# GpSimd forms the low mantissa bits of eleven weight tiles, and the second chunk's first layer is issued ahead of the first chunk's second layer

## The chip, the cores and the metric

The kernel runs on one core of one Trainium2 chip. The metric is the device time of one execution in microseconds (us); the lower the better. The core's engines are named as the profile names them: PE (TensorE, with PEld for its weight loads), DVE (VectorE), ACT (ScalarE), POOL (GpSimd), and SP, which only issues DMAs here. Each engine takes its instructions strictly in the order in which they were written for it.

## What is computed

Attention with a local window and global tokens, then a gated feed-forward layer ("MoE" in the names, though there is one expert):

```python
# batch 8, heads 8, 512 local + 32 global tokens, head size 64
s_g  = q_g @ concat(k_g, k_l).T / 8          # global queries see all keys
s_ll = where(|i - j| <= 32, q_l @ k_l.T / 8, -1e9)
s_l  = concat(q_l @ k_g.T / 8, s_ll)         # local queries: window + global keys
out  = concat(softmax(s_g) @ v, softmax(s_l) @ v)
x    = out as 4608 tokens x 512
xn   = x / sqrt(mean(x*x) + 1e-6) * rms_g
y    = (silu(xn @ w_gate) * (xn @ w_val)) @ w_out     # 512 -> 2 x 1536 -> 512
```

The attention inputs are float32. The three weight matrices are float64 and reach the chip as raw 64-bit words.

## The kernel before, in words

**Chunks.** The tokens are worked on in nine chunks: chunk c (0 to 7) is the 512 local tokens of batch c, chunk 8 all 256 global tokens. A chunk needs its attention, its root-mean-square norm, its first layer (the products with w_gate and w_val, in 12 slices f of 128 columns) and its second layer (the product with w_out). Matrix products of the feed-forward part are made in float16 with each operand split into a high and a low half, three products for one. Chunks 2 to 8 use fewer products, with sums of weight blocks ("folds") that the kernel forms once during chunks 0 and 1, stores to DRAM and fetches for each chunk. Chunks 0 and 1 use the weights as they lie in SBUF.

**Weights.** The 18 tiles of weights (0 to 11: slices of w_gate and w_val; 12 to 17: w_out) are turned from float64 into two float16 halves on the chip, each by this chain, in which the letter is the step's name in the order and the number behind it the tile:

- W: two DMAs of 512 KB each bring the raw 64-bit words.
- m (`rebias`): two instructions of 128x512 multiply the upper word, read as a float32, by 2^-112, on DVE for the tiles in `MULT_V` and on ACT for the others.
- s (`shift`): DVE shifts all 1024 words left by 3.
- the three lowest bits, from the lower word's upper half (two instructions of 128x512 16-bit numbers with a step of 8 bytes): step k (`three`) on ACT for the tiles in `LOW_A`, step l (`low`) on DVE for the others.
- g (`sign`): two DVE instructions of 128x512 put sign, shifted word and the three bits together. Their two inputs both lie in SBUF.
- q: ACT squares the tile and sums the squares; p: PE adds these sums up; e: some small DVE instructions make the tile's power-of-two scales from them (for two tiles at a time from tile 2 on: p2 and e2 are of tiles 2 and 3, p3 and e3 of tiles 4 and 5, and so on).
- a: ACT writes the high half (128x1024); d: DVE writes the low half (128x1024).

**The first chunks' other steps.** Attention unit u (0 to 3 belong to chunk 0, 4 to 7 to chunk 1): L and V load it, S makes the scores on PE, M (eight DVE instructions of 128x128) adds the mask and takes the maximum, E (eight on ACT) the exponentials, T (PE) and C (ACT) turn them round, A (PE) multiplies by the values, R and X (DVE) divide, Q (ACT) squares, Z (DVE) sums squares. Then for chunk 0 or 1: N (13 small DVE instructions in a chain: the inverse root), D (four on DVE), U (PE turns and scales the tokens, four parts), H (ACT) and Y (DVE) the high and low halves. I f.wi: first-layer products of chunk 0, slice f, matrix w, half i (six matmuls of 128x512); B (ACT tanh), b, h (DVE) the gate, c (ACT) and r (DVE) its two halves; O i.j: second-layer products of chunk 0, o its results. J, j, u, w: folds. K: the scale of w_out. Steps with a leading 1 (1:P0 to 1:P71, R, w) are those of chunk 1: P0 to P47 are its first layer, P48 to P71 its second. Steps such as 1:S/0+1 are attention of a later chunk.

**Order.** `JOBS` lists the steps of chunk 0 as they are set up; the program first only notes every instruction under a name like `0:M2.1.3` (chunk:step.part). Then

```python
    for name in ORDER.split() or list(plan):
        for call in plan.pop(name):
            call()
```

writes all 3692 noted parts in the order of the list `ORDER`, which was made ahead of time and stands in the file. What `ORDER` says for one engine is that engine's queue. `PAGES` and `BANKS` say in the same manner which of the 43 SBUF pages (128x1024 floats), 8 wide ones and 8 PSUM banks each tile takes. A tile framework adds the waits between engines.

Of the kernel before, what the change touches and what calls it, by code (L numbers as in the profile page):

```python
# [71 lines left out]
0:l1.1 0:g1.0 0:g1.1 0:q1.0 0:z3.0 0:z4.1 0:T3.1.0 0:z4.0 0:R0.0 0:S1.0 0:M1.0.3 0:M1.0.1 0:M1.0.0
0:M1.0.2 0:V2.0 0:M1.1.1 0:M1.1.0 0:C2.1.0 0:M1.1.2 0:E1.0.0 0:M1.1.3 0:z4.2 0:R2.0 0:z2.2 0:m0.0
0:m0.1 0:s0.0 0:A0.0 0:l0.0 0:m3.0 0:E1.1.0 0:g0.0 0:m3.1 0:k3.0 0:l0.1 0:T1.1.0 0:V1.0 0:T1.0.0
0:p1.0 0:A2.0 0:s3.0 0:X0.0 0:g3.0 0:C1.0.0 0:Q0.0 0:g0.1 0:q0.0 0:T3.0.0 0:C1.1.0 0:g3.1 0:V3.0
0:X2.0 0:z2.3 0:p0.0 0:e0.0 0:e0.1 0:e0.2 0:z5.0 0:C3.0.0 0:Q2.0 0:z6.0 0:W2.0 0:C3.1.0 0:e1.0
0:q3.0 0:R3.0 0:A1.0 0:R1.0 0:Z0.0 0:e1.1 0:z6.1 0:W4.0 0:Z2.0 0:z6.2 0:X1.0 0:A3.0 0:a0.0 0:X3.0
0:Q1.0 0:e1.2 0:L4.0 0:Z1.0 0:Q3.0 0:Z3.0 0:N0.0.0 0:N0.1.0 0:N0.2.0 0:N0.3.0 0:N0.4.0 0:N0.5.0
0:N0.6.0 0:m2.0 0:s2.0 0:N0.7.0 0:k2.0 0:N0.8.0 0:N0.9.0 0:N0.10.0 0:N0.11.0 0:N0.12.0 0:g2.0 0:D0.1
0:W7.0 0:a1.0 0:D0.2 0:D0.3 0:m4.0 0:W5.0 0:W6.0 0:D0.0 0:U0.3.0 0:U0.0.0 0:d0.0 0:g2.1 0:e0.3  # L80
0:s4.0 0:U0.1.0 0:k4.0 0:d1.0 0:g4.0 0:q2.0 0:H0.1.0 0:U0.2.0 0:H0.0.0 0:g4.1 0:m7.1 0:S4.0 0:m5.0
0:k5.0 0:Y0.1.0 0:q4.0 0:Y0.0.0 0:H0.3.0 0:e1.3 0:p2.0 0:m7.0 0:H0.2.0 0:M4.0.0 0:e2.0 0:M4.0.2
0:e2.1 0:a2.0 0:m6.0 0:s7.0 0:s5.0 0:e0.4 0:g5.1 0:e2.3 0:k6.0 0:L5.0 0:g5.0 0:q5.0 0:Y0.3.0
# [18 lines left out]
0:d11.0 0:g12.0 0:g12.1 0:I10.00.0 0:V7.0 0:I10.01.0 0:b8.0 0:I11.00.0 0:C4.0.0 0:k16.0 0:h8.0
0:q12.0 0:g14.0 0:B9.0 0:R4.0 0:B10.0 0:s16.0 0:g16.0 0:K0.1 0:g17.1 0:q17.0 0:S7.0 0:b9.0 0:g16.1
0:e6.5 0:I11.10.0 0:b10.0 0:C4.1.0 0:M7.1.3 0:q16.0 0:g14.1 0:M7.0.1 0:M7.1.2 0:I11.01.0 0:I10.10.0
0:I10.11.0 0:I11.11.0 0:V4.0 0:h9.0 0:q14.0 0:K0.2 0:K0.3 0:h10.0 0:K1.0 0:K2.0 0:K2.1 0:E5.0.0
0:K2.2 0:a12.0 0:S6.0 0:M7.1.0 0:T5.0.0 0:M7.0.0 0:M7.1.1 0:C5.0.0 0:M6.0.1 0:T5.1.0 0:c4.0 0:d12.0
0:A4.0 0:d12.1 0:O0.3.0 0:M7.0.3 0:K2.3 0:M7.0.2 0:r3.0 0:M6.1.2 0:B11.0 0:C5.1.0 0:M6.1.0 0:M6.1.1
# [6 lines left out]
0:r10.0 0:C7.1.0 0:A7.0 0:r9.0 0:O4.0.0 1:w0.0 0:C6.0.0 0:Z4.0 0:J1.0 0:K2.4 0:X7.0 0:O3.1.0 1:w6.2
0:O4.2.0 0:C6.1.0 0:O4.1.0 0:d17.1 0:X5.0 0:V6.0 0:A6.0 0:d17.0 0:O5.1.0 0:Q5.0 0:O4.3.0 0:Q7.0
0:Z5.0 0:Z7.0 0:X6.0 1:w0.1 0:Q6.0 0:O5.2.0 0:J0.3 1:w12.1 0:Z6.0 0:N1.0.0 0:N1.1.0 0:N1.2.0
0:N1.3.0 0:N1.4.0 0:N1.5.0 0:N1.6.0 0:N1.7.0 0:O5.3.0 0:O5.0.0 0:N1.8.0 0:N1.9.0 0:N1.10.0 0:N1.11.0
0:N1.12.0 0:D1.1 0:D1.0 0:D1.3 0:D1.2 0:U1.0.0 1:w24.0 0:H1.0.0 0:Y1.0.0 0:U1.1.0 0:U1.2.0 0:U1.3.0
0:H1.1.0 0:Y1.1.0 0:o2.0 0:H1.3.0 1:P8.0 1:P0.0 0:Y1.3.0 0:H1.2.0 0:Y1.2.0 1:P1.0 1:R1.0 1:P9.0
# [2208 lines left out]
```

## Time and profile before

| | |
|---|---|
| time, median of 3 runs | 895.82 us (894.6 to 896.01) |
| the profiled execution | 896.6 us, its span 894.8 us |
| PE busy | 866.1 us, 97% of the span |
| DVE / ACT / POOL busy | 705.4 / 551.1 / 271.6 us |

The profile's page gives busy times over the span and in 40 slices of it; other views list waits, instructions in order of time, and busy times by stretch. An engine's instructions overlap a little, so the time that one costs its queue is read from one start to the next: two starts 0.39 us apart cost 0.39 us each, though each may be shown as lasting 0.48 us.

### The profile page before, as it was taken

Reading aid. Unit: us, or ns where it says so; the run is one execution under the profiler, and the core shown is the slowest. Engines: PE = TensorE matmul, PEld = TensorE weight load, DVE = VectorE, ACT = ScalarE, POOL = GpSimd, SP = SyncE. Lnnn points to the kernel's source line nnn. Section 1 sums busy time; section 2 is a strip of 40 time slices with the busy share of each in tenths; the row PEclk is TensorE's granted clock in tenths of the full one; section 3 lists DMA queues with packets and bytes.
Section 4 is the critical chain, followed back from the end, with each engine's and each line's share of the span. In section 5 each row is a group of like instructions: output and inputs, shape, how many; then the busy total and the mean of one; then the engine's idle time right before and its main releaser. Section 6 shows DMA issues by size and latency. Waiting matters only on the chain.

```text
span 894.8 us, 27793 instructions
## 1 busy us (share of the span) xinstructions
PE 866.1 (97%) x11430; PEld 665.6 (74%) x11430; DVE 705.4 (79%) x1831; ACT 551.1 (62%) x1341; POOL 271.6 (30%) x244
## 2 busy tenths in 40 slices
PE   5699999999999999999999999999999999999998
PEld 3554455545548885688888888888888888888887
DVE  6899999798686777777886899779877798598445
ACT  6999993657344754566474876577575863456222
POOL 0000000024834575415431264132431443125402
PEclk9699999999999999999999999999999999999999
DMA  9994340498975988974797476967986859638412
GB/s 349 406 401 179 97 140 25 141 284 284 377 236 163 317 271 257 310 232 146 261 379 243 135 256 226 323 257 256 295 317 217 260 186 343 224 113 277 153 48 94
DMA packets 101006, 212.03 MB, mean 237 GB/s; under 512 B 8080, under 2 KB 34448, under 8 KB 100880
## 3 DMA queue, kind: packets, MB, share of 16 engines
...
## 4 chain that ended last, share of the span: by engine, by line
PE 88%; DVE 4%; ACT 1%; issue 1%; DVEq 0%; ACTq 0%
PE bank L2088 88%; DVE page L2088 4%; ACT page L2088 1%; DVE wide L2088 0%; DVE xg L2088 0%; DVE ws L2088 0%; DVE hs L2088 0%; DVE sm L2088 0%; DVE pow L2088 0%; DVE half_inv L2088 0%; DVE gsm L2088 0%; DVE c_h L2088 0%; DVEq L2088 0%; DVE nt L2088 0%; ACTq L2088 0%
## 5 line engine op out<-in xcount | busy, mean ns | idle before, releaser
L2088 PE MATMUL bank<-page,page 128*128 128x256 f16 (+6 forms) x8226 | 726.0, 279 | 19.9 <-ACT page L2088 9.0
L2088 PEld LDWEIGHTS <-page 128*128 128x128 f16 (+1 forms) x5340 | 512.4, 98 | 164.8 <-issue 10.4
L2088 POOL TENSOR_TENSOR page<-page,page 128x512 f16<-128x512 f32 (+5 forms) x155 | 175.5, 1150 | 302.8 <-ACT page L2088 279.2
L2088 DVE TENSOR_TENSOR page<-bank,page 128x512 f32<-128x512 f32 x158 | 106.7, 683 | 59.9 <-PE bank L2088 36.5
L2088 ACT CAST page<-page 128x512 f16<-128x512 f32 (+1 forms) x142 | 108.1, 784 | 69.0 <-DVE page L2088 55.2
L2088 ACT COPY page<-bank 128x512 f32<-128x512 f32 (+3 forms) x158 | 82.0, 543 | 107.0 <-PE bank L2088 92.8
L2088 ACT ACTIVATE page<-page,sm 128x128 f32<-128x128 f32 x344 | 126.5, 391 | 26.2 <-DVE sm L2088 21.3
L2088 DVE TENSOR_TENSOR page<-page,page 128x256 f32<-128x256 f32 (+4 forms) x159 | 97.1, 626 | 10.1 <-ACT page L2088 8.0
L2088 POOL TENSOR_TENSOR page<-page,sm 128x512 f32<-128x512 f32 x22 | 25.5, 1168 | 209.0 <-DVE sm L2088 201.1
L2088 ACT ACTIVATE page<-page 128x512 f32<-128x512 f32 (+2 forms) x93 | 77.0, 905 | 9.6 <-DVE page L2088 7.2
L2088 DVE CUSTOM_DVE_ANT_0 page<-bank,page 128x128 f32<-128x128 f32 x248 | 60.4, 282 | 19.2 <-PE bank L2088 17.9
L2088 PEld LDWEIGHTS bank<-page,page 64*32 64x32 f32 (+4 forms) x3120 | 55.2, 112 | 25.0 <-ACT page L2088 10.8
L2088 PE MATMUL bank<-wide,page 32*64 32x96 f32 (+6 forms) x2042 | 62.4, 267 | 0.9 <-issue 0.9
L2088 DVE TENSOR_TENSOR page<-page 128x256 f32<-128x256 f32 (+3 forms) x116 | 60.1, 532 | 1.2 <-PE bank L2088 0.2
L2088 PE MATMUL bank<-page,wide 128*128 128x256 f16 (+2 forms) x496 | 60.9, 276 | 0.0
L2088 PEld LDWEIGHTS <-wide 128*128 128x128 f16 x462 | 44.7, 98 | 13.6 <-issue 0.8
L2088 ACT ACTIVATE page<-page,half_inv 128x512 f32<-128x512 f32 x58 | 40.0, 718 | 18.4 <-DVE page L2088 16.4
L2088 DVE SCALAR_TENSOR_TENSOR page<-page,page 128x512 f32<-128x512 f32 x58 | 42.8, 752 | 8.5 <-ACT page L2088 8.0
L2088 DVE SCALAR_TENSOR_TENSOR page<-page,c_h,page 128x512 f32<-128x512 f32 x65 | 48.6, 767 | 0.6
L2088 ACT ACTIVATION_READ_ACCUMULATOR page<-page,sm 128x1 f32 x248 | 46.9, 189 | 0.0
L2088 ACT ACTIVATE page<-bank,half_inv 128x512 f32<-128x512 f32 (+1 forms) x36 | 21.5, 612 | 35.4 <-PE bank L2088 35.4
L2088 POOL TENSOR_TENSOR wide<-page,wide 128x512 f16<-128x512 f32 (+2 forms) x23 | 25.0, 1098 | 42.1 <-ACT wide L2088 42.1
...
## 6 DMA issues: line engine op xcount, KB each, us to landing
page<-wd SPq DMA_DIRECT2D x112, 512.0 KB, 7.4
...
```

What stands on the lines that cost most here:

```text
L2088: return lambda *a, **k: write(self.engine, lambda: call(*a, **k))
```

## The change

**Who makes the three low bits.** The tiles 2, 3, 4, 5, 6, 9, 10, 11, 13, 14 and 16 get them from POOL (a new step y, `floor`, with the same arithmetic that ACT used); the tiles 7, 12 and 15 from ACT, where DVE did it; 0, 1, 8 and 17 stay on DVE. The rebias m of the tiles 3, 7, 11 and 12 goes from DVE to ACT.

```diff
-    MULT_V = (0, 1, 3, 7, 11, 12)
-    LOW_A = (2, 3, 4, 5, 6, 9, 10, 11, 13, 14, 16)
+    MULT_V = (0, 1)
+    LOW_A = (7, 12, 15)
+    LOW_P = (2, 3, 4, 5, 6, 9, 10, 11, 13, 14, 16)
...
+        def floor():
+            for _, _, _, raw in raws:
+                half = raw.bitcast(I16).rearrange("p (n t) -> p n t", t=4)
+                nc.gpsimd.tensor_scalar(
+                    half[:, :, 2], half[:, :, 1], 2.0**-13, -0.5 + 2.0**-14, ALU.mult, ALU.add
+                )
+
...
-        third = ("k", three) if i in LOW_A else ("l", low)
+        third = ("k", three) if i in LOW_A else ("y", floor) if i in LOW_P else ("l", low)
```

In `JOBS` only the letters of these steps change. `ORDER`, `PAGES` and `BANKS` are new lists; so the queues of all engines change, in the whole program. No other instruction is added, removed or changed. The queues' beginnings (steps of chunk 0 without their leading 0, and a part that is 0 left out: `M2.1` is M2.1.0):

PE, before:

```
S0 S2 S3 z1 T0.0 T0.1 T2.0 T2.1 z3 T3.1 S1 A0 T1.1 T1.0 p1 A2 T3.0 p0 z5 A1 A3 U0.3 U0.0 U0.1 U0.2
S4 p2 I0.00 I1.00 I0.10 I1.10 I0.11 I0.01 I1.11 I1.01 p3 I2.00 I2.01 p4 I2.10 I2.11 S5 I3.00 I3.10
I3.11 I3.01 I4.00 I4.10 I4.11 p5 I4.01 I5.00 ...
```

PE, after:

```
S2 z1 S3 S0 T2.0 z3 T3.1 T2.1 S1 T3.0 T0.0 T0.1 A0 z5 p1 A2 T1.0 T1.1 A3 A1 p0 S5 U0.0 U0.1 U0.2
S4 U0.3 I1.00 I1.10 I0.10 S7 p2 I1.01 I0.00 I0.01 I0.11 I1.11 I2.00 I2.01 p3 I3.00 S6 I3.10 I3.11
I2.10 I3.01 I2.11 T4.1 I5.10 I5.11 T5.1 T5.0 T4.0 p4 I4.10 ...
```

Later on PE, before: I11.11, K1, then all of O (with T, A of the units 4 to 7 between), U1, then 1:P. After: the I steps with T, A of the units 4 to 7 between, U1 among the last of I10, then 1:P12, P24, P2 and so on; K1 comes behind 33 steps P, and the O steps stand among and behind the last P of the first layer. The steps d of the tiles 12 to 17, which the O steps need, move back with them on DVE, as do several c and r.

DVE, before, from unit 1's mask on:

```
M1.1.3 z4.2 R2 z2.2 m0 m0.1 s0 l0 m3 g0 m3.1 l0.1 s3 X0 g3 g0.1 g3.1 X2 z2.3 e0 e0.1 e0.2 z6 e1 R3
R1 Z0 e1.1 z6.1 Z2 z6.2 X1 X3 e1.2 Z1 Z3 N0.0 ... N0.6 s2 N0.7 ... N0.12 g2 D0.1 D0.2 D0.3 D0 d0
g2.1 e0.3 s4 d1 g4 g4.1 m7.1 Y0.1 Y0.0 e1.3 m7 M4.0 ... d2 ...
```

DVE, after, from the same place on:

```
M1.1 M1.1.3 e1 e1.1 z6 e1.2 z6.1 z6.2 X2 M1.1.1 g0 g0.1 Z2 e1.3 R0 X0 R1 d1 s3 g3 g3.1 X3 Z0 X1 Z3
Z1 N0.0 ... N0.12 D0 D0.2 D0.3 e0 e0.1 D0.1 s2 e0.3 M5.0.1 M5.1.3 d0 Y0.1 M4.1.1 Y0.0 M4.1.3 M4.0.2
g2.1 M5.0 M4.1.2 M4.0 M5.1.1 g2 M4.1 M4.0.1 M4.0.3 Y0.3 M5.1.2 M5.0.3 Y0.2 e0.2 M7.0 M7.1.1 M5.1 e2
M7.1.3 M7.1.2 e0.4 e2.1 M7.0.3 s4 e2.3 g4.1 s5 g4 d2 e2.2 g5 s6 g5.1 M7.0.2 M5.0.2 M7.0.1 d3 ...
```

ACT, before:

```
z0 E0.0 E2.1 E0.1 E2.0 E3.1 C0.0 E3.0 C2.0 C0.1 q1 C2.1 E1.0 E1.1 k3 C1.0 Q0 q0 C1.1 C3.0 Q2 C3.1
q3 a0 Q1 Q3 m2 k2 a1 m4 k4 q2 H0.1 H0.0 m5 k5 q4 ...
```

ACT, after:

```
z0 E2.1 E2.0 E3.1 E3.0 E0.0 E0.1 C2.0 C2.1 C0.0 C0.1 q1 C3.0 C3.1 E1.0 a1 m3 Q2 E1.1 Q0 C1.0 C1.1
Q3 Q1 q0 m4 m2 a0 H0.1 H0.0 H0.2 q3 m5 H0.3 m6 q2 E4.1 E4.0 a2 a3 E5.1 q4 m9 B1 q5 ...
```

POOL, after, from its start: y3.1 y3 y2.1 y2 y4.1 y4 y6 y5 y6.1 y5.1 y9 y9.1 y10 y10.1 y11 y11.1 y16.1 y16 y14 y13.1 y13 y14.1, then what it did before. The loads on SP come as L2 L3 L0 W1 L1 W0 V0 V2 W3 V3 V1 L5 W4 W2 L4, where they came as L0 L2 L3 L1 W1 V0 W0 W3 V2 V1 V3 W2 W4 L4.

## Rows read from the trace of the kernel before

**Rows 1.** The page: busy time of all engines, and busy tenths of POOL and TensorE's granted clock in 40 slices of 22.4 us.

```profile
PE 866.1 (97%) x11430; PEld 665.6 (74%) x11430; DVE 705.4 (79%) x1831; ACT 551.1 (62%) x1341; POOL 271.6 (30%) x244
...
POOL 0000000024834575415431264132431443125402
PEclk9699999999999999999999999999999999999999
```

**Rows 2.** Busy time by stretch. Columns: stretch, its length, busy us (and instructions) of PE, PEld, DVE, ACT, POOL, granted clock, DMA share, GB/s.

```profile
66.00:116.80 50.80, 50.80 (x387) 24.79 (x374) 50.00 (x112) 50.46 (x93) 0.00 (x0) 1.00 0.46 158
116.80:175.00 58.20, 58.20 (x711) 32.73 (x711) 52.14 (x151) 36.52 (x95) 0.81 (x1) 1.00 0.26 84
...
267.50:894.80 627.30, 619.17 (x8476) 530.77 (x8473) 472.14 (x1170) 358.39 (x881) 228.04 (x206) 1.00 0.70 234
```

**Rows 3.** Two of PE's waits over the whole span: whom it waited for, us in total, times, longest.

```profile
PE bank L2088 <- ACT page L2088: 13.0, 6, 7.4
...
PE bank L2088 <- issue: 3.0, 3, 1.7
```

**Rows 4.** PE in order of time: start, length, instructions of one form merged, idle time before them and who ended it. The row at 40.09 is U0 and S4, p2 follows it, the one at 47.17 is I0 and I1 (eight steps of six), the one at 109.10 is a step S.

```profile
40.09 6.51 PE L2088 MATMUL bank<-page,page 128*128 128x128 f32 x96 [7.43 <-ACT page L2088]
...
47.17 10.58 PE L2088 MATMUL bank<-page,page 128*128 128x512 f16 x48
...
61.40 0.38 PE L2088 MATMUL bank<-ssq,ones 128*128 128x2 f32 x2 [0.52 <-ACT page L2088]
...
65.83 10.31 PE L2088 MATMUL bank<-page,page 64*32 64x128 f32 x104 [0.71 <-DVE page L2088]
...
109.10 1.16 PE L2088 MATMUL bank<-page,page 64*32 64x128 f32 x64
```

**Rows 5.** ACT in order of time: k3 at 25.06 (C1.0 follows it), q3 at 31.41 with its accumulator's read (a0 follows at 32.46), Q1, Q3, m2 and k2 from 33.49, a1 at 37.84, H0.1 and H0.0 at 44.66.

```profile
25.06 2.50 ACT L2088 ACTIVATE page<-page 128x512 int16<-128x512 int16 x2
27.31 0.69 ACT L2088 COPY page<-bank 128x512 f32<-128x512 f32 x1
...
31.41 1.05 ACT L2088 ACTIVATE page<-page 128x1024 bf16<-128x1024 f32 x1
...
32.46 1.13 ACT L2088 ACTIVATE page<-page,ws 128x1024 f16<-128x1024 f32 x1
33.49 4.59 ACT L2088 ACTIVATE page<-page 128x512 f32<-128x512 f32 x6
```

**Rows 6.** DVE in order of time: g3 and g0.1 at 26.43, e0 at 30.39, Z1 and Z3 at 34.14, N0 from 35.45 (s2 inside it at 36.74), g2 at 38.40, D0 at 39.07, d0 at 39.85, d1 at 42.44, Y0.1 and Y0.0 at 45.38.

```profile
26.43 2.08 DVE L2088 SCALAR_TENSOR_TENSOR page<-page,ends,page 128x512 int32<-128x512 int32 x3 [0.78 <-ACT page L2088]
...
30.39 0.16 DVE L2088 TENSOR_SCALAR pow<-bank 128x1 int32<-128x1 int32 x1 [0.98 <-PE bank L2088]
...
34.14 1.28 DVE L2088 TENSOR_REDUCE ss<-page 128x4 f32<-128x512 f32 x2
35.45 0.17 DVE L2088 TENSOR_REDUCE rn<-ss 128x4 f32<-128x16 f32 x1
...
36.74 0.69 DVE L2088 TENSOR_SCALAR page<-page 128x1024 int32<-128x1024 int32 x1
...
38.40 0.75 DVE L2088 SCALAR_TENSOR_TENSOR page<-page,ends,page 128x512 int32<-128x512 int32 x1
39.07 0.87 DVE L2088 TENSOR_SCALAR page<-ident,rn 128x128 f32<-128x128 f32 x4
39.85 1.28 DVE L2088 SCALAR_TENSOR_TENSOR page<-page,ws,page 128x1024 f16<-128x1024 f32 x1
...
42.44 1.28 DVE L2088 SCALAR_TENSOR_TENSOR page<-page,ws,page 128x1024 f16<-128x1024 f32 x1
...
45.38 1.41 DVE L2088 SCALAR_TENSOR_TENSOR page<-bank,gvec,page 128x512 f16<-128x512 f32 x2
```

**Rows 7.** Groups of instructions in the first 135 us, by form: count, busy us, mean ns of one, idle time before them. In order: step k, exponentials (E) and rebias with squares (m, Q) on ACT; the mask steps M, step l and the rebias m on DVE.

```profile
L2088 ACT ACTIVATE page<-page 128x512 int16<-128x512 int16 x22 | 27.6, 1392 | 0.0
L2088 ACT ACTIVATE page<-page,sm 128x128 f32<-128x128 f32 x64 | 24.7, 392 | 0.9 <-PE bank L2088 0.9
...
L2088 ACT ACTIVATE page<-page 128x512 f32<-128x512 f32 x28 | 17.2, 675 | 0.1
...
L2088 DVE CUSTOM_DVE_ANT_0 page<-bank,page 128x128 f32<-128x128 f32 x64 | 15.6, 282 | 7.6 <-PE bank L2088 7.6
...
L2088 DVE TENSOR_SCALAR page<-page 128x512 uint16<-128x512 uint16 x14 | 10.2, 746 | 0.0
...
L2088 DVE TENSOR_SCALAR page<-page 128x512 f32<-128x512 f32 x10 | 4.2, 425 | 0.0
```

**Rows 8.** POOL over the whole span, by form: its instructions of 128x512 floats with one large input, and those of 128x256 with two.

```profile
L2088 POOL TENSOR_TENSOR page<-page,sm 128x512 f32<-128x512 f32 x22 | 25.5, 1168 | 209.0 <-DVE sm L2088 201.1 <-ACT sm L2088 4.9 <-issue 2.5
...
L2088 POOL TENSOR_TENSOR page<-page,page 128x256 f16<-128x256 f32 x26 | 19.1, 741 | 6.6 <-ACT page L2088 6.6
```

**Rows 9.** One form of DVE instruction with two inputs in SBUF, first in the first 135 us (POOL idle), then from 175 us to the end (POOL at work); and one such instruction in order of time, with what POOL did beside it.

```profile
L2088 DVE TENSOR_TENSOR page<-page,page 128x512 f16<-128x512 f32 x8 | 5.3, 683 | 0.2 <-ACT page L2088 0.2
...
L2088 DVE TENSOR_TENSOR page<-page,page 128x512 f16<-128x512 f32 x34 | 25.9, 770 | 4.8 <-ACT page L2088 4.5
...
305.69 1.45 DVE L2088 SCALAR_TENSOR_TENSOR page<-page,page 128x512 f32<-128x512 f32 x1
...
305.31 1.27 POOL L2088 TENSOR_TENSOR page<-page,page 128x512 f32<-128x512 f32 x1 [0.73 <-ACT page L2088]
```

More of the change, by code (lines that the diff above doesn't have):

```diff
@@ L72 @@
[L72 to L83, printed above, removed]
@@ L102 @@
[L102 to L107, printed above, removed]
@@ L114 @@
[L114 to L119, printed above, removed]
@@ new lines @@
+1:w56.0 1:w12.2 1:w12.4 1:w0.0 0:q14.0 1:w0.1 0:r9.0 1:R28.0 1:M2/0+1.0 1:N2/0+1.1 0:K0.2 0:K0.3
+1:E2/0+1.0 1:R4.0 1:M0/0+1.0 0:K1.0 1:N0/0+1.1 1:F2/0+1.0 1:w0.3 1:w0.2 0:r7.0 1:w0.4 1:F1/0+1.0
+0:K2.0 1:P34.0 1:D2/0+1.0 1:P39.0 1:P35.0 0:K2.1 0:K2.2 1:P44.0 1:P45.0 0:a16.0 1:GL/1+1.0 1:w30.0
+0:a14.0 0:d16.0 1:M3/0+1.0 0:d16.1 1:D1/0+1.0 1:P42.0 0:a15.0 0:d14.0 1:R23.0 1:N3/0+1.1 0:d15.0
+0:a12.0 1:R41.0 0:d14.1 0:d12.1 0:d12.0 0:d15.1 1:E3/0+1.0 1:F3/0+1.0 1:P30.0 1:R12.0 0:O0.2.0
+1:R35.0 1:w12.3 1:D1/0+1.1 1:P31.0 1:w30.1 1:T1/0+1.0 1:R45.0 0:a13.0 0:d13.0 1:R46.0 0:O0.1.0
@@ new lines @@
+0:d13.1 1:P43.0 0:O1.2.0 1:D3/0+1.0 0:O0.3.0 1:R42.0 1:E0/0+1.0 1:F0/0+1.0 1:w30.3 0:O1.1.0
+1:D0/0+1.0 1:R37.0 1:R16.0 1:R17.1 1:P46.0 0:O1.3.0 1:w14.0 1:w15.0 1:D0/0+1.1 1:R38.0 1:w17.0
+1:D2/0+1.1 1:T0/0+1.0 1:w44.0 1:P47.0 1:D3/0+1.1 1:T3/0+1.0 1:R13.1 1:w2.0 1:R39.0 1:R24.0 1:R43.0
+1:T2/0+1.0 0:O2.2.0 1:R25.1 1:R31.0 1:R20.0 1:R47.0 1:A/0+1.0 1:B/0+1.0 2:w0.0 1:R29.1 0:O3.2.0
+1:GV/1+1.0 0:K2.3 1:X/0+1.0 1:X/0+1.1 1:Y/0+1.0 1:Y/0+1.1 1:GS/1+1.0 1:GM/1+1.0 1:GM/1+1.1
+1:GM/1+1.2 0:O0.0.0 0:O1.0.0 1:GT/1+1.0 1:L/2+1.0 1:GN/1+1.0 1:GN/1+1.1 1:GN/1+1.2 2:w0.1 1:w57.0
@@ new lines @@
+1:R5.1 2:w2.0 1:GT/1+1.2 1:R21.1 1:GT/1+1.1 1:GT/1+1.3 1:w30.2 0:O2.0.0 1:R8.0 1:w3.0 1:R9.1
+1:S/2+1.0 1:M0/2+1.1 1:N0/2+1.1 1:M0/2+1.0 2:w2.1 1:w38.0 1:N0/2+1.0 1:w38.1 1:M2/2+1.0 0:O3.0.0
+1:w38.3 1:Y/0+1.2 1:w38.2 1:M1/2+1.0 0:a17.0 1:E0/2+1.0 1:F0/2+1.0 1:w30.4 1:M1/2+1.1 0:O2.3.0
+1:D0/2+1.0 1:M3/2+1.0 1:N1/2+1.1 1:D0/2+1.1 1:w24.0 1:N2/2+1.0 0:O2.1.0 0:O4.2.0 1:N1/2+1.0 1:w32.0
+1:w59.0 1:R36.0 0:O4.0.0 1:w24.1 2:GL/1+1.0 1:w46.0 1:M2/2+1.1 0:K2.4 0:O3.1.0 1:M3/2+1.1 1:w24.3
+1:w38.4 1:N3/2+1.1 0:d17.0 1:w33.0 1:P48.0 1:R40.0 0:O3.3.0 1:E1/2+1.0 1:X/0+1.2 1:P60.0 1:N2/2+1.1
@@ new lines @@
+1:w24.2 0:d17.1 2:w2.2 1:P49.0 1:N3/2+1.0 1:V/2+1.0 0:O5.2.0 1:P66.0 1:E2/2+1.0 1:F2/2+1.0 1:w5.0
+1:P61.0 1:P67.0 1:D2/2+1.0 1:w24.4 1:w26.0 1:w27.0 0:O5.0.0 1:w18.0 1:R44.0 1:w40.0 1:T0/2+1.0
+1:w18.1 0:O4.3.0 0:O5.3.0 1:w18.3 1:GA/1+1.0 1:w18.2 1:w18.4 1:w20.0 1:R48.0 1:w35.0 0:O4.1.0
+1:w21.0 1:F1/2+1.0 1:L/0+2.0 1:D2/2+1.1 0:o2.0 1:w23.0 1:D1/2+1.0 1:R32.0 1:D1/2+1.1 0:O5.1.0 0:o3.0
+0:o2.1 1:P50.0 1:T2/2+1.0 1:R37.1 1:P62.0 1:GN/1+1.3 1:E3/2+1.0 1:T1/2+1.0 1:F3/2+1.0 1:GD/1+1.0
+1:w29.0 2:w11.0 1:Y/0+1.3 1:D3/2+1.0 0:o1.0 1:D3/2+1.1 1:T3/2+1.0 1:A/2+1.0 1:B/2+1.0 2:L/2+1.0
@@ new lines @@
+3:N1/0+2.0 3:w44.0 3:M3/0+2.1 3:n44.0 3:O21.0 3:F2/0+2.0 3:t38.3 3:n44.1 3:n44.2 3:M1/0+2.0
+3:M3/0+2.0 3:E3/0+2.0 3:N3/0+2.0 3:N0/0+2.1 3:O31.0 3:F3/0+2.0 3:n44.3 3:n44.4 3:O24.0 3:t40.1
+3:w46.0 3:M0/0+2.0 3:M1/0+2.1 3:D2/0+2.0 3:O25.0 3:n44.5 3:n44.6 3:n44.7 3:n44.8 4:w11.0 3:O26.0
+3:E1/0+2.0 5:w31.0 3:t46.1 3:O22.0 3:O32.0 3:t33.1 3:t45.2 3:V/0+2.0 3:E0/0+2.0 3:F0/0+2.0 3:n44.9
+3:n44.10 3:n44.11 3:n44.12 3:n44.13 3:n46.0 3:D0/0+2.0 3:D3/0+2.0 3:D2/0+2.1 3:w53.0 3:O33.0
+3:F1/0+2.0 3:n47.0 3:O27.0 3:n47.1 3:O28.0 3:O29.0 3:D0/0+2.1 3:O23.0 3:R56.0 3:n46.1 3:D1/0+2.0
```

699 lines of the change are left out of this document (347 added, 352 removed), and 18 rows, old and new, of the table BANKS.

## Prediction, made before the changed kernel was timed

> **What bounds the kernel now.** The page comes first: PE is busy 866.1 of 894.8 us [rows 1]. PE is the bound, no PE instruction is taken away, and so the change can win only from the 28.7 us in which PE stands idle, or lose by making new idle time. The view of PE's waits says where those 28.7 us are: 13.0 of them, in six pieces, were ended by ACT, and one piece alone is 7.4 [rows 3]. PE in order of time puts that piece at 40.09 us, ahead of U0, the step that turns chunk 0's normed tokens; a short wait of 0.52 for ACT follows at 61.40 and one of 0.71 for DVE at 65.83 [rows 4]. In the stretch from 66 to 116.8 us PE has no gap at all (50.80 of 50.80), and from 267.5 on 619.17 of 627.30 [rows 2]. The first product of the feed-forward part starts at 47.17 [rows 4]. So the place to look at is the head, up to some 66 us: what stands between the loads and that first product.
>
> The busy times by stretch say who is slow there: between 66 and 116.8 us DVE works 50.00 and ACT 50.46 of 50.80 us, POOL not at all [rows 2]; POOL's first work falls into the ninth slice, behind 174 us [rows 1]. The clock line has a 6 in the second slice, 22.4 to 44.8 us [rows 1]: in part of it TensorE ran at the lower of its two levels, after idling for U0.
>
> **What the change costs, part by part.**
>
> *Step y on POOL.* ACT gives up 22 k (2 x 11 tiles). Two took 25.06 to 27.31 us [rows 5], so 1.12 us each, 25 us in all; ACT gains six k for the tiles 7, 12 and 15 (6.7) and eight m of 0.68 (5.4) [rows 7]: 12.5 us less. DVE gives up eight m of 0.425 and six l of 0.746 [rows 7]: 7.9 us by these means, less where they overlap. POOL gets 22 y. No such instruction is in the trace; the nearest is POOL's 128x512 form with one large input, 1.17 us, below it the 128x256 form, 0.74 [rows 8]. As ACT takes 1392 ns for this strided 16-bit form against 675 ns for an ordinary one [rows 7], twice 1.17, 2.34, is the upper end. I take 1.17, the row of equal shape: 22 x 1.17 = 26 us. [...]
>
> *What POOL does to DVE.* Steps g and d read two inputs in SBUF. One such form took 683 ns while POOL idled and 770 ns from 175 us on, where POOL was busy 228.04 of 627.30 us, 36% [rows 2, 9]: 0.09 us each. In the worst row one took 1.45 us with a POOL instruction beside it [rows 9]. Up to d4 POOL has 13 y, 15 us in some 37 us, 41%; about 15 such DVE steps fall into it, 0.1 us each, 1.5 us in all. The lower end is 0, the upper one 13 x 1.17 = 15 us, if each y blocks DVE for its length. [...] The row of 1.45 us shows the clash; the mean of 770 shows that it rarely costs that much, so the row near the mean decides for me.
>
> *A: U0's start, -1.5.* U0 needs D0, which needs the chain N0 (35.45 to 39.07 with s2 and g2 in it [rows 6]), which needs the last sums of squares of chunk 0, on ACT and DVE. ACT's queue ahead of its last Q loses k3 (2.25) and q0 and q3 (1.05 each), gains m3 (1.35), and has a1 for a0: 3.0 us less [rows 5, 7]. DVE's queue to N0 loses m3 (0.85) and e0 (0.5) and gains d1 (1.28) [rows 6, 7]: level. Its waits of 0.78 for k3 and 0.98 for e0's sums [rows 6] have no place left, but with ACT early DVE paces, and new waits for Q2 or PE may come; of the 1.76 I take 0.6, ends 0 and 1.76. Between N0.0 and D0's end s2 (0.6) and g2 (0.67) go out, two small e (0.4) come in: -0.9. U0 then starts at 38.6 instead of 40.09. One new wait must not bite: g3 waits for y3 on POOL. ACT's queue up to m3 holds, against that up to k3 before, C3.0, C3.1 (0.69 each) and a1 (1.13) more and four E (0.39 each) less [rows 5, 7], +0.9, so m3 starts near 26.0, ends at 27.4, and y3 at 29.7 with 1.17 each. DVE reaches g3 seven steps ahead of N0.0 (two g of 0.7, five X and Z of 0.66 [rows 6]), 34.85 - 4.7 = 30.2. It fits by half a microsecond; with 2.34 each DVE would lose 1.8.
>
> *B: U0 to the first product, -2.2.* Before: 47.17 - 40.09 = 7.08, with DVE working through d0, g2, s4, d1, two g4, m7 and two Y (39.85 to 46.8) while Y is what the product needs [rows 4, 6]. After, DVE has s2 (0.6), e, two M (0.28 each), d0 (1.2), Y, one M, Y (0.7 each): 4.2 us. But the M between the two Y reads S4's scores, and S4 stands behind three of U0's four parts. U0 and S4 took 6.51 at the lower clock [rows 4]; four fifths are 5.2, and M and Y behind it make 6.2; with half of it at the full clock 4.7 to 5.5. I take 5.5: -1.6. Also S5 (1.16 us [rows 4]) is now done while PE waits for U0, and p2 (47.17 - 46.60 = 0.57) goes behind the first products: another -0.6 of PE work left behind the start.
>
> *C: the first layer of chunk 0, -0.4.* The waits at 61.40 and 65.83, with one of 0.18 later, are 1.4 [rows 4]. In the new order two steps are tight. p3 needs q5, which needs g5.1: DVE has from Y0.0 on 17 M (4.0), six g (4.0), two Y (1.4), three s (2.0), d2 (1.2), small e (0.7), 13.3 with 0.7 of POOL's interference 14.0, then q5 1.05: 15.05. PE has ten I steps of 10.58 / 8 = 1.32, S7 and p2: 14.9. That is level: 0 to 1.5, taken 0.5. The same count up to d4, which the I4 steps need, is 28.9 against 29.2: taken 0.5. New waits 1.0 for 1.4 old ones.
>
> *D: all later, 0, ends -1.5 and +3.* From 116.8 on DVE has 6 and ACT 22 us to spare in 58 [rows 2], so O's low halves d12 to d17, moved back, find time, all the more as O itself is moved back. PE waits little there: 3.0 us for issue in all [rows 3]. Chunk 2's norm chain gets less PE work as cover, 8 us instead of 10 for some 7.4 us of chain: enough by my count, not by much.
>
> **The sum.** -1.5 - 2.2 - 0.4 + 0 = -4.1. The profiled execution took 896.6 (span 894.8), so 892.5 of its kind; it lies 0.8 above the median of the runs, 895.82, from which the change gives **891.7 us**.
>
> **The rivals.** *R1, slower: y locks DVE.* For it: DVE is nearly full up to 135 us, the row of 1.45 us, and C's steps are level, so that what DVE loses PE waits for. Against: 770 against 683. With 0.65 us per y for 13 y, 8.5 less the 1.5 counted, PE waits 7 us more: 898.7; with the whole 1.17, 15.2 - 1.5 = 13.7: 905. It decides from about 4 us, 0.45 us per y, upward. Chance 0.15. *R2, no change: DVE paces.* ACT's lead is worth nothing, y3 or S4 takes the place of what ACT held up: A gives -0.5, B -0.6, the rest nothing, 894.7. For it: DVE is as full as ACT. Chance 0.20. *R3: the new order brings waits later on* (p3, d4, chunk 2's norm, or the second layer for the late d12 to d17) of 3 to 5 us: 895 to 897. For it: such margins of 0.3 and 0.6 us; a list made ahead carries its planner's costs. Chance 0.12, a quarter of it slower by over 0.2%. *R4, more is won:* U0 meets the full clock, B is 4.0 instead of 5.5 and no new wait comes: 891.7 - 1.5 - 1.0 = 889.2. Chance 0.10. *R5, the change does not do what it says:* y takes 2.34, g2, g4 and g5 wait for POOL in place of ACT, and 22 x 2.34 = 51 us of POOL work run beside DVE: 896 to 900. Chance 0.05.
>
> **How the numbers follow.** The forecast has 0.38, with 889.5 to 893.9 as its own range (A and B each by a microsecond, C by 0.5). A measurement of this kernel tells about 0.2%, 1.8 us, from no change. Faster takes the forecast and R4 (0.48), a quarter of R2 and 0.02 of R3: 0.55. Slower takes R1, R5 and 0.03 of R3: 0.23. The same: 0.22. The range holds 8 in 10 if it reaches from R4, less a little, to the near part of R1: 888 to 898.5.
>
> **What would show it.** Right: U0 starts near 38.6 and the first I step near 44; the k group on ACT has 6 instructions; POOL shows 22 y of about 1.2 us from some 26 us on; g and d lengthen by a tenth; PE shows less than 1.5 us of waits between 45 and 116. Wrong: g's mean near 1.1 us or more, or DVE's waits naming POOL (R1, R5); a PE wait of microseconds ended by DVE before p3 or I4, or behind 260 us (R3); the wait for U0 as long as before (R2).

## The result, and the profile after

The changed kernel takes 906.93 us in the median (904.93 to 907.24), the kernel before 895.25 us beside it: a ratio of 1.0125, 95% interval 1.0107 to 1.0144. The forecast was 891.7, the range 888 to 898.5; the time lies on the other side of the kernel before and out of the range, near R1's upper figure. The profiled execution has a span of 905.5 us, 10.7 more than before.

The page of the changed kernel: busy times, and the slices of PE, POOL and the granted clock.

```profile
PE 873.0 (96%) x11430; PEld 670.2 (74%) x11430; DVE 707.7 (78%) x1817; ACT 537.8 (59%) x1333; POOL 300.7 (33%) x266
...
POOL 0341201033326566324531155213531335024402
PEclk9599999999999999999999999999999999999999
```

POOL works from the second slice on, as meant, ACT has 13 us less to do, PE has the same 11430 instructions. Yet PE is busy 873.0 instead of 866.1 us [rows 1], 6.9 more for the same work, and idle 3.7 us more. Busy time by stretch (first the columns' stretch and length, then PE, PEld, DVE, ACT, POOL, clock, DMA): the head is cut where the first product of the feed-forward part starts.

```profile
22.00:50.80 28.80, 20.41 (x383) 17.30 (x383) 23.33 (x61) 17.36 (x42) 8.86 (x6) 0.53 1.03 402
50.80:66.00 15.20, 14.32 (x141) 7.03 (x140) 14.85 (x59) 14.01 (x41) 7.35 (x6) 1.00 1.01 364
66.00:300.00 234.00, 232.33 (x2509) 128.85 (x2514) 197.23 (x476) 147.31 (x347) 67.53 (x54) 1.00 0.58 188
300.00:905.50 605.50, 593.74 (x8062) 507.11 (x8061) 458.38 (x1136) 343.94 (x848) 216.74 (x197) 1.00 0.71 237
```

Before, the first product started at 47.17 [rows 4], now at 50.81: 3.6 us of the loss. Between 22 us and that product the mean clock is 0.53; the clock's records show two levels, 1.00 and 0.50 of full speed, and put the lower one from 21.5 to 48.8 us, where before it held from 23.0 to 29.8 and from 36.6 to 43.5. Behind 50.8 us PE idles 0.88, 1.67 and 11.76 us in the three stretches (length less busy time), 14.3 in all, against 9.6 before counted in the same manner: 4.7 us more. Some 2.4 us are left, of which a second piece of low clock (3.4 us at 0.50, from 451.6 on, behind a wait of 2.86 us) can hold at most 1.7, the half of it.

Where the head loses is seen with DVE and POOL side by side. DVE of the changed kernel from N0 on: three of D0's instructions at 39.09, then e0 and the fourth, s2, d0, Y0.1.

```profile
36.50 0.17 DVE L2097 TENSOR_REDUCE rn<-ss 128x4 f32<-128x16 f32 x1
...
39.09 2.83 DVE L2097 TENSOR_SCALAR page<-ident,rn 128x128 f32<-128x128 f32 x3
41.58 0.35 DVE L2097 TENSOR_SCALAR pow<-bank 128x1 int32<-128x1 int32 x1
...
42.05 1.29 DVE L2097 TENSOR_SCALAR page<-ident,rn 128x128 f32<-128x128 f32 x1
42.99 0.89 DVE L2097 TENSOR_SCALAR page<-page 128x1024 int32<-128x1024 int32 x1
...
44.34 1.54 DVE L2097 SCALAR_TENSOR_TENSOR page<-page,ws,page 128x1024 f16<-128x1024 f32 x1
47.51 0.75 DVE L2097 SCALAR_TENSOR_TENSOR page<-bank,gvec,page 128x512 f16<-128x512 f32 x1 [1.63 <-ACT page L2097]
```

POOL of the changed kernel up to 60 us: y3, then y2 and y4, then y6 and y5.

```profile
26.34 3.21 POOL L2097 TENSOR_SCALAR page<-page 128x512 int16<-128x512 int16 x2 [25.90 <-ACT page L2097]
39.11 5.96 POOL L2097 TENSOR_SCALAR page<-page 128x512 int16<-128x512 int16 x4 [9.56 <-ACT page L2097]
52.57 5.68 POOL L2097 TENSOR_SCALAR page<-page 128x512 int16<-128x512 int16 x4 [7.50 <-ACT page L2097]
```

The group of all y, count, busy us and mean ns in the middle:

```profile
L2097 POOL TENSOR_SCALAR page<-page 128x512 int16<-128x512 int16 x22 | 31.8, 1447 | 112.0 <-ACT page L2097 88.8 <-ACT xg L2097 16.4 <-DVE page L2097 5.8
```

y2 starts at 39.11, in the same instant as D0. Before, D0's four instructions took 0.87 us together [rows 6]; now the last of them ends at 43.34, 4.2 us behind the first one's start. Single ones took 1.42 us (0.28 before). PE shows what it cost:

```profile
40.57 0.80 PE L2097 MATMUL bank<-page,page 128*128 128x128 f32 x2 [1.04 <-DVE page L2097]
43.40 10.16 PE L2097 MATMUL bank<-page,page 128*128 128x128 f32 x106 [2.03 <-DVE page L2097]
```

U0 can begin at 40.57 with the first blocks of D0 and stops till 43.40 for the last.

To put a number on it for whole runs, I add up an **excess**: for each DVE instruction beside which a POOL instruction ran, its length less the median length of the same operation on the same tiles and shape with POOL idle. In the first 135 us it is 0 before and some 9 us after (9.1; 8.3 to 9.4 by the runs from which the medians are taken; the expectations below call it 8.6): D0 3.4, s 1.9, g 1.7, e 1.0, a subtraction of the folds 0.6, d 0.5. The steps M, X, Y, b and h, which read PSUM, and Z show none (beside y M took 0.27 to 0.29 us, 0.28 without; Y 0.74, 0.75 without; X, b, h and Z 0.67 to 0.75, as without). It is all length: none of DVE's waits in these 135 us was ended by POOL. And DVE is busy 707.7 us here, 699.8 in the run without y below. Later, where POOL worked before too, the kernel before has some 28 us of such excess, yet its PE waits for DVE only 2.3 us in the whole run.

### The profile page after: what moved, and what is told of

Its sections match the earlier page's. It is cut to its first block, busy times and chain, and to the rows that moved or that the text cites. A ratio compares the mean times of both kernels' runs of the same rounds, so it can differ in the third digit from the quotient of the medians.

```text
span 905.5 us, 27844 instructions
## 1 busy us (share of the span) xinstructions
PE 873.0 (96%) x11430; PEld 670.2 (74%) x11430; DVE 707.7 (78%) x1817; ACT 537.8 (59%) x1333; POOL 300.7 (33%) x266
## 4 chain that ended last, share of the span: by engine, by line
PE 50%; DVE 3%; DMA 1%; issue 1%; ACT 0%; POOL 0%; SPq 0%; ACTq 0%; DVEq 0%
PE bank L2097 50%; DVE page L2097 2%; DVE wide L2097 1%; DMA page<-in_qkb_dram 1%; DMA page<-wb 0%; ACT page L2097 0%; POOL page L2097 0%; SPq L2097 0%; DVE sm L2097 0%; ACTq L2097 0%; DVEq L2097 0%
## 5 line engine op out<-in xcount | busy, mean ns | idle before, releaser
L2097 PE MATMUL bank<-page,page 128*128 128x256 f16 (+5 forms) x8338 | 755.5, 285 | 18.2 <-DMA page<-in_qk_dram 6.9
L2097 PEld LDWEIGHTS <-page 128*128 128x128 f16 (+1 forms) x5514 | 529.6, 98 | 178.0 <-issue 14.4
L2097 POOL TENSOR_TENSOR page<-page,page 128x512 f16<-128x512 f32 (+4 forms) x170 | 190.2, 1136 | 345.0 <-ACT page L2097 233.0
L2097 ACT CAST page<-page 128x512 f16<-128x512 f32 (+1 forms) x151 | 115.9, 794 | 93.1 <-DVE page L2097 86.5
L2097 DVE TENSOR_TENSOR page<-page,page 128x256 f32<-128x256 f32 (+5 forms) x165 | 98.4, 605 | 11.9 <-ACT page L2097 10.3
L2097 PE MATMUL bank<-wide,page 32*64 32x96 f32 (+7 forms) x2040 | 72.4, 264 | 5.3 <-issue 2.9
L2097 DVE CUSTOM_DVE_ANT_0 page<-bank,page 128x128 f32<-128x128 f32 x256 | 61.7, 283 | 15.8 <-PE bank L2097 14.3
L2097 POOL TENSOR_SCALAR page<-page 128x512 int16<-128x512 int16 x22 | 31.8, 1447 | 112.0 <-ACT page L2097 88.8
L2097 ACT ACTIVATE page<-page 128x512 f32<-128x512 f32 (+2 forms) x83 | 62.0, 787 | 11.4 <-DVE page L2097 10.5
L2097 DVE SCALAR_TENSOR_TENSOR page<-page,page 128x512 f32<-128x512 f32 x64 | 48.8, 771 | 11.2 <-ACT page L2097 11.1
L2097 ACT ACTIVATE page<-bank,half_inv 128x512 f32<-128x512 f32 (+1 forms) x36 | 21.5, 611 | 39.7 <-PE bank L2097 39.6
L2097 ACT ACTIVATE page<-bank,kk 128x512 f32<-128x512 f32 (+1 forms) x24 | 15.7, 658 | 39.3 <-PE bank L2097 39.0
L2097 PE MATMUL bank<-page,wide 128*128 128x256 f16 (+2 forms) x340 | 38.2, 270 | 0.0
```

The source lines that it names most:

```text
L2097: return lambda *a, **k: write(self.engine, lambda: call(*a, **k))
```

## The experiments

Theory 1: y on POOL shuts DVE out, and the time goes there. Theory 2: the new order itself, with its clock and its waits, is slow.

**Holding POOL back behind D0.** A POOL memset of one element of N0's tile, which must wait for D0's last reader, ahead of y2 in POOL's queue.

```diff
         for call in plan.pop(name):
             call()
+        if name == "0:D0.1":
+            now.gpsimd.memset(chunks[0]["rn"][:, 1, 1:2], 0.0)
```

> The changed kernel with one POOL instruction more, a one-element memset that must wait for the last of D0's four DVE instructions and stands ahead of y2 in POOL's queue; so no y runs beside D0. Theory 1 (y locks DVE): in the changed kernel D0's four instructions took 39.10 to 43.34 us instead of 0.9 us, beside y2 and y4; here they take 0.9 again, U0 starts about 3.3 us earlier and the time falls by 2 to 3.5, to 903.5 to 905 us. Theory 2 (the new order with its low clock and its waits costs the 11 us, the lock is hidden by something else): within 1 us of the changed kernel, 906 to 908.

Measured 901.60 us, ratio to before 1.0067 (1.0052 to 1.0082): 5.3 us less than the changed kernel, for one instruction more. D0 on DVE:

```profile
39.99 0.68 DVE L2098 TENSOR_SCALAR page<-ident,rn 128x128 f32<-128x128 f32 x3
...
40.84 0.28 DVE L2098 TENSOR_SCALAR page<-ident,rn 128x128 f32<-128x128 f32 x1
```

and the first product on PE:

```profile
47.62 1.24 PE L2098 MATMUL bank<-page,page 128*128 128x512 f16 x5
```

D0 is back at its old length and the product 3.2 us earlier. The gain is more than the 2 to 3.5 us that Theory 1 was to bring. The rest of it, 2.1 us, was not traced to its place; the lower level held for 17.1 us of the head instead of 27.3.

**No y at all.** The body of `floor` is empty: the low three bits of eleven tiles are not formed.

> The changed kernel without its 22 instructions y: the low three mantissa bits of eleven weight tiles are not formed, everything else and the order are the same. Theory 1: all locks go (9 us of DVE time in the first 175 us by the trace, some 5.7 of it ahead of the first 66 us), the time falls by 4 to 7, to 900 to 903 us. Theory 2: within 2 us of the changed kernel, 905 to 908; the rest of the loss is the order's.

Measured 898.19 us, 1.0035 (1.0023 to 1.0048): 8.7 of the 11.7 us are gone, the excess in the first 135 us is 0, the first product at 46.45. So in the new order the presence of y costs 8.7 us, more than Theory 1 was to bring (900 to 903). What remains, 2.5 us, comes with the new order. PE idles 7.0 us behind 66 us in this run, 4.6 before (sums of the waits in PE's order of time); one wait of 1.98 for DVE, treated below, and an issue wait of 2.43 are the largest. But the two profiled executions, 896.95 and 896.6, lie only 0.4 us apart, so these sums don't yet account for 2.5 us between the medians.

**y on ACT in the new order.** In `floor` the instruction is `now.scalar.activation(...)` with the same arithmetic, at the same places of the list.

> The changed kernel and order with the 22 y issued on ACT at the same places of the list (as before's k: 1.12 us each). Theory 1: D0 takes 0.9 us again, U0 starts some 3 us earlier; but ACT gets 25 us of work back in an order that has no room for it, so that the first layer waits for ACT: 903 to 912. Theory 2: ACT's load comes on top of an order that is slow already: 910 to 918.

Measured 916.01 us, 1.0227 (1.0210 to 1.0245). The first product starts earliest of the runs so far, 46.02, but then ACT is late (p3's sums wait 3.45 us for it at 69.29): the new order does need somebody else to make these bits. Both theories lose a part: no lock, and still slower.

**y on POOL in the old order.** In `three` the 22 instructions of the eleven tiles go to POOL; all else as before.

> The kernel before and its order with the 22 k of the eleven tiles issued on POOL instead of ACT, nothing else moved. Theory 1: y2 falls beside s2, g2 and D0 and the later y beside g and d: ACT's relief (-1 to -2 us) is eaten by the locks, 895 to 899. Theory 2: POOL's help is worth what it takes off ACT, 892 to 895.

Measured 912.74 us, 1.0190 (1.0174 to 1.0205), slower than either theory said, and 17 us slower than before with no step moved. The excess in the first 135 us is 18.2 us (the expectation for the pieces below calls it 18.9). POOL's y2 and y4 now fall on the norm chain; POOL there:

```profile
38.50 5.90 POOL L676 TENSOR_SCALAR page<-page 128x512 int16<-128x512 int16 x4 [10.58 <-ACT page L2091]
```

DVE (N0.1, N0.2 and N0.3 in the first row, N0.7 in the second), and PE at U0:

```profile
38.83 2.45 DVE L2091 TENSOR_SCALAR rn<-rn 128x4 f32<-128x4 f32 x3
...
43.14 1.02 DVE L2091 TENSOR_TENSOR rn<-rn 128x4 f32<-128x4 f32 x1
```

```profile
46.74 6.33 PE L2091 MATMUL bank<-page,page 128*128 128x128 f32 x96 [10.37 <-DVE page L2091]
```

N0.7, on 128x4 numbers and 0.16 us long when alone, took 1.02 us, and N0.1 1.03 instead of 0.17, small as they are. In the changed kernel three of D0's instructions end with the y that they meet, at 40.52, 41.92 and 43.34, the y at 40.44, 41.84 and 43.26. Of two more rows there, the first, on one number per partition, lies inside a y (41.92 to 43.26) and is not held; the second, on two and 0.17 us long when alone, meets a y (108.40 to 109.74) and ends at 109.76.

```profile
41.98 0.15 DVE L2097 TENSOR_SCALAR ws<-pow 128x1 int32<-128x1 int32 x1
...
108.76 1.00 DVE L2097 TENSOR_SCALAR ws<-pow 128x2 int32<-128x2 int32 x1
```

Theory 1 stands, in a worse form than I gave it.

**D0 on ACT.** The four instructions of D0 as `now.scalar.mul(dg[0][:, g, :], ident, y[:, g : g + 1])`, y2 and y4 beside them.

> The changed kernel with D0's four blocks made by ACT instead of DVE (ACT idles from 38.9 to 42.2 us in the changed kernel), y2 and y4 beside them as before. If only DVE is locked out, and ACT is not: D0 takes some 1.4 us instead of 4.2 and U0 starts 2 to 3 us earlier, 902 to 905 us, about what the run with POOL held back behind D0 gave, and ACT's four instructions show no lengthening beside y. If POOL's reads hold up every engine, ACT's four take over 1 us each and the time stays at 906 to 908.

Measured 904.55 us, 1.0094 (1.0079 to 1.0110), 2.4 less than the changed kernel. ACT's four took 0.40 us and 0.97 for three, beside y2 or not: ACT wasn't shut out here. The gain is smaller than by holding POOL back, since q0, now behind D0.0 in ACT's queue, starts at 39.91 instead of 35.66, and PE's p0 and S5, which stand ahead of U0, wait for it (7.07 us, up to 41.09).

**y in four pieces.** Each y as four instructions of 128 columns, first in the new order, then (with y on POOL) in the old one.

```diff
-                nc.gpsimd.tensor_scalar(half[:, :, 2], half[:, :, 1], ...)
+                for n in range(0, 512, P):
+                    nc.gpsimd.tensor_scalar(half[:, n : n + P, 2], half[:, n : n + P, 1], ...)
```

> The changed kernel with each y instruction cut into four of 128 columns; same data, same places. If DVE is shut out for the length of one POOL instruction: y pieces of some 0.4 to 0.5 us, so a DVE instruction of the kinds that are locked waits 0.5 us at most instead of 1.3; D0's four take 1.5 to 2.5 us instead of 4.2 and the sum of the excess in the first 135 us falls from 8.6 to 3 to 6 us: 902 to 905. If POOL keeps DVE out for a whole queue of its work, or cutting makes y much longer: 906 to 910.

> The kernel before and its order with y on POOL in four pieces each, against 912.7 us with whole y. If DVE loses the length of the POOL instruction that it meets: the excess of 18.9 us in the first 135 us falls to 6 to 10 and the time to 901 to 906. If the loss comes from tiles that are ready later on POOL than on ACT: 912 to 918, since the pieces take longer in sum.

New order: 903.51 us, 1.0091 (1.0076 to 1.0107), 3.4 less than with whole y. Old order: 905.07 us, 1.0104 (1.0089 to 1.0120), 7.7 less. D0 on DVE in the new order:

```profile
40.11 1.14 DVE L2108 TENSOR_SCALAR page<-ident,rn 128x128 f32<-128x128 f32 x3
...
41.38 0.42 DVE L2108 TENSOR_SCALAR page<-ident,rn 128x128 f32<-128x128 f32 x1
```

and POOL's group of all pieces:

```profile
L686 POOL TENSOR_SCALAR page<-page 128x128 int16<-128x128 int16 x88 | 54.8, 622 | 90.0 <-ACT page L2108 64.9 <-ACT xg L2108 12.8 <-DVE page L2108 6.6
```

POOL needs 54.8 instead of 31.8 us for the same bits, and the kernel is faster: three of D0's instructions took 1.14 us beside pieces of 0.62 in the mean, where single ones had taken 1.42 beside y of 1.33. The excess in the first 135 us is 3.6 us (new order, some 9 whole) and 6.6 (old order, 18.2 whole). It shows how much DVE is held, not what the kernel loses. In the old order 18.2 us of excess go with 17.1 us of lost time, but 6.6 with 9.2: with pieces DVE also waits 5.0 us for POOL's results, which are late. In the new order 6.4 us of excess (POOL held back) stand 3.4 us above the run without y, 5.0 (D0 on ACT) 6.4, and 3.6 (pieces) 5.3.

**POOL writes without reading.** Each y replaced by `nc.gpsimd.memset(half[:, :, 2], 0)`: the low bits come out as zero.

> The changed kernel with each y replaced by a POOL memset of the same 128x512 16-bit places: POOL writes and doesn't read, and the low three bits come out as zero. If it is POOL's reading that shuts out DVE's second input: g and d beside it keep 0.75 and 1.28 us, while D0, s and the small scalar instructions may still be held. If any POOL instruction shuts DVE out: excess for both kinds. The time lies between the run without y (898) and the changed kernel (907), at 898 to 903, lower the shorter the memset is.

Measured 906.06 us, 1.0136 (1.0105 to 1.0167); it was to be 898 to 903. POOL's four memsets in the place of y2 and y4:

```profile
39.20 4.63 POOL L2095 MEMSET page<- 128x512 int16 x4 [10.04 <-ACT page L2095]
```

DVE's D0.1 and s2 beside them and, later, two forms with two inputs: a d beside a memset of 63.91 to 65.27, and a subtraction of the folds beside one of 95.57 to 96.83.

```profile
39.15 4.76 DVE L2095 TENSOR_SCALAR page<-ident,rn 128x128 f32<-128x128 f32 x1
39.34 5.10 DVE L2095 TENSOR_SCALAR page<-page 128x1024 int32<-128x1024 int32 x1
...
64.05 1.27 DVE L2095 SCALAR_TENSOR_TENSOR page<-page,ws,page 128x1024 f16<-128x1024 f32 x1
...
95.89 0.41 DVE L2095 TENSOR_TENSOR page<-page 128x256 f32<-128x256 f32 x1
```

D0.1 is held for all four memsets in a row, 4.76 us; s2's 5.10 is mostly its turn behind D0.1. The d, 1.28 us when alone and 1.48 and 1.54 beside y in the changed kernel, keeps its length beside a memset; so does the subtraction, 1.05 us beside y there. So in these rows a POOL that only writes held the TENSOR_SCALAR from SBUF to SBUF (4.76 us for 0.28 alone) and left the two forms with a second input at their length (1.27 and 0.41), where y, which reads too, lengthened all three (D0.1 to 1.29, the two others as above).

**The late wait.** PE waits 1.98 us for DVE at 535 us in the changed kernel, as long at 525.6 without y, and 1.97 at 530.8 with POOL held back: y doesn't make this wait. First R33, then GD were moved ahead of t29.1 and t29.0, all of chunk 4, in DVE's queue, POOL held back behind D0 in both.

> The run with POOL held back behind D0, and chunk 4's step R33 ahead of t29.1 and t29.0 in DVE's queue. In that run PE waits 1.97 us at 530 us, just until R33 ends, and R33 stands behind t29.1 and t29.0, which took 1.02 and 1.15 us beside POOL where 0.41 is usual without. If R33's place behind them is the cause, PE's wait falls below 0.5 us and the time by 1 to 2 us, to 899.5 to 900.5. If not, the wait stays at 1.9 to 2.0 and the time at 901.6.

> The run with POOL held back behind D0, and chunk 4's step GD ahead of t29.1 and t29.0 in DVE's queue. With R33 moved, PE's wait at 530 us still ended when GD did, 530.4 us, so GD's bank is what PE waits for. If that is so, the wait of 1.97 us falls below 0.5 and the time by about 1.5 us, to 899.5 to 900.7. If something else is late next, the wait keeps more than half of its length and the time stays at 901 to 902.

With R33 moved: 902.68 us, 1.0089 (1.0073 to 1.0105), the wait 1.60. With GD moved: 903.17 us, 1.0084 (1.0068 to 1.0101), the wait 1.21. Both have new waits of 0.4 and 0.35 us at 549 to 551. (GD's result lies in the quarter of a page from which t29 still reads, so here t29 gets wrong values; the instructions are the same.) Neither paid, against what was expected: neither is faster than the 901.60 of the run on which they were built. Part of the wait goes, and what was moved back is waited for next. What makes the 2.5 us of the order is so not settled.

**All three repairs**: y in pieces, POOL held back behind D0, GD moved (with the same wrong t29).

> The changed kernel with the three repairs together: each y in four pieces, POOL held back behind D0, GD ahead of t29.1. If the locks are what separates the changed kernel from the run without y (898.2), and the late wait is 1.5 us of the rest: 897 to 900 us. If pieces only spread the same lost time: 901 to 903.

Measured 907.19 us, 1.0129 (1.0114 to 1.0145), outside what was expected: nothing is left of the gains. POOL, held back and with 54 us of pieces to make, is now late itself: DVE waits 4.0 us for it, the longest wait 3.1, and p3's sums wait 3.70 us at 65.23, for an ACT that waits for the chain y, g, q. The repairs aren't additive.

**PE kept busy.** 92 matmuls that nobody reads, in PE's gaps of the changed kernel's head; 94 in the kernel before; there also with H0 and Y0 moved ahead of d1.

```diff
+        at, n = WARM.get(name, (0, 0))
+        for _ in range(n):
+            now.tensor.matmul(banks[at][:, :256], ident16[:, :P], ident16, start=True, stop=True)
```

> The changed kernel with 92 matmuls more that nobody reads (128x256 float16, into a bank about to be overwritten) in the seven gaps of PE ahead of U0. It asks what the low clock costs: in the changed kernel the records show the lower level from 21.5 to 48.8 us. If the clock stays high and PE's slowness is on the path: U0, S4 and the first product follow each other in some 4.5 us instead of 7.4, 902 to 904.5 us. If DVE sets the pace there whatever the clock, or the extra work doesn't raise it: 905.5 to 908.

> The kernel before with 94 such matmuls in its three gaps of PE ahead of U0 (20, 23 and 33 to 40 us). U0 and S4 then take 3.5 us at the upper level instead of 6.5, but the first product waits for Y on DVE, which is busy without a gap from 35.5 to 47 us: within 1 us of before, 894.5 to 896.5. If PE's clock is on the path there, 2 to 3 us faster, 892.5 to 893.5.

> The same, with H0.1, H0.0 and Y0.1, Y0.0 moved ahead of d1 in the order (ACT's q2 and DVE's d1, two g4 and m7.1 come behind them). If DVE's queue is what the first product waits for in the kernel before, it starts about 2.5 us earlier and the time falls to 892.5 to 894; part is given back if d1, moved back by 1.4 us, makes the second slice wait. If not, 895 to 897.

912.43 (1.0185, 1.0165 to 1.0206), 912.87 (1.0182, 1.0159 to 1.0205) and 915.28 us (1.0213, 1.0194 to 1.0232), all outside what was expected. In the first the head does what the clock theory said: the lower level for 3.4 us instead of 27.3, the first product at 47.53 instead of 50.81, with D0 still held: U0 and what follows it took 4.1 us from 43.42 on at the upper level, 7.4 from 43.40 on in the changed kernel, at the lower one up to 48.8. So in the head the run with the higher clock, 3.3 us earlier at the first product, gives back as much as the one with the freed D0 (3.2 us, above). But 9 us are lost behind the first product: PE is busy 4.5 us longer there and idles 4.5 us longer, 3.1 of it in issue waits, which end with nothing that the profile shows; the lower level comes back for 10.2 us, behind waits of 4.16 and 1.98 us. PE's waits in the second run:

```profile
PE bank L2088 <- issue: 14.7, 7, 3.7
```

and one of them in order of time:

```profile
36.12 0.26 PE L2088 MATMUL bank<-page,page 128*32 128x64 f32 x1 [3.26 <-issue]
```

14.7 us of issue waits, against 3.0 before [rows 3], though the steps in which they fall are the old ones, up to 500 us behind the added matmuls. They rose in the first run too, from 4.3 us in the changed kernel to 8.8. As an answer on the clock the last two are void. What makes these waits was not shown.

**The old head reordered without POOL.** s2 and g2.0 behind D0, U0's parts in order, H0 and Y0 ahead of d1.

> The kernel before, k on ACT as it was, with its head reordered alone: s2 and g2.0 behind D0 instead of inside the norm chain, U0's parts in the order 0, 1, 2, 3, and H0.1, H0.0, Y0.1, Y0.0 ahead of d1. It asks whether the head of the old kernel can be shortened without POOL. If the chain to U0 and Y is what counts: the first product starts at 44 to 45 us instead of 47.17 and the time falls by 1 to 2.5, to 893 to 894.5. If DVE's and ACT's whole load up to 66 us counts, PE waits later for what was put back: within 1 us of before.

Measured 895.41 us, 1.0005 (0.9996 to 1.0015): the same. The first product starts at 47.58; PE then waits 1.32 us where it waited 0.71 [rows 4]. No run beats the kernel before.

## Why the prediction was wrong

**What POOL does to DVE** is the step that failed. It priced 15 two-input instructions (g and d) at 0.1 us, 1.5 us in all, and put every other DVE instruction at nothing, without a reason. Measured: some 9 us of excess in the first 135 us, and 8.7 us of time that go when y goes. For g and d the price was near: 2.2 us in all, a mean of 804 ns for 748 and of 1316 for 1281, no more than the tenth that it gave as its sign, though the few that were held lost 0.2 to 0.8 us each. What was left out made the loss: D0, s and e, tensor_scalar from SBUF with a single large input, and the subtraction of the folds, 6.9 us together, up to 1.1 us for each meeting. D0 alone took 3.4 us more, and it stands on the very chain that I had found to set U0's start. And of the 1.5 us only 0.7 entered the sum, in C; A and B, in whose stretch D0, s2 and d0 lie, have nothing for it. The signs named for this failure, g's mean near 1.1 us or DVE's waits naming POOL, did not show either, for D0 was held within its own length. R1 named the mechanism and gave 898.7, or 905 at its end; it got 0.15.

That each y blocks DVE for its whole length, as that upper end had it, no run shows: 13 x 1.17 = 15 us were named for 13 y, and the excess is some 9 us beside the 19 y of the first 135 us. Single rows come to it: D0's 1.42 us beside y of 1.33, 0.28 when alone, and N0.1's 1.03 us in the old order, 0.17 when alone.

The lock is not the whole miss. Without y the kernel still takes 898.19 us, 6.5 above the forecast: there the first product starts 0.7 us earlier than before (46.45 for 47.17) where A and B had 3.1, and what follows lost some 3 us.

**A** forecast U0 at 38.6; it began at 40.57 and went on at 43.40. Without y it began at 39.90, so A was worth 0.2 us of 1.5. ACT's lead was worth next to nothing, as R2 had it: ACT idles 2.4, 3.2 and 3.4 us for DVE and PE between 31 and 47 us, N0 starts at 36.50 instead of the 34.85 forecast, later than before (35.45, [rows 6]). A g0 of 1.56 us beside y3 stands ahead of it, but made little of this: counted from each run's first matmul, N0 starts 30.8 us after it, 30.5 without y and 29.3 before. In that stretch DVE is busy 25.6 us without y and 24.5 before, where A had its queue as level, and idle 5.0 and 4.8, where A had 0.6 us of its waits go: two waits as long as the old ones came instead, 0.91 for PE and 0.86 for ACT. y itself was near its price, 1.33 us when undisturbed, 1.45 in the mean, for 1.17 taken.

**B** had the right wait: the M between the two Y did wait for S4 (1.5 us, up to 49.80). But with the clock at 0.50 until 48.8 us U0's start to the first product took 7.4 us from 43.40, not 5.5; without y, 6.55 from 39.90. The 6.51 us of U0 and S4, which B scaled, were read as at the lower clock, but the level had risen to 1.00 at 43.5, half-way through them. That the lower level would hold for 27.3 us instead of 6.8 and 6.9 was in none of the rivals; PE had idled 1.20 and 1.85 us before it fell at 21.5, and 0.95, 1.14, 3.22, 1.04 and 2.03 us while it stayed low, and with 92 matmuls in such gaps it was low for 3.4 us of the head.

**C and D**: waits of 0.88 and 0.31 us, 1.2 in all for the 1.0 forecast, so C came as it was counted. D was put at 0; without y the whole order is 2.5 us slower than the kernel before although the head is 0.7 ahead, which is about D's bound of +3. Chunk 2's norm cost nothing visible; which step does is open.

The chances went wrong in the way of the sum: 0.55 on faster rested on the mean of one form, and R1 was weighed by that same mean, though neither it nor its row of 1.45 us is a row of the forms that lost most.
